# Q and K of an attention and SwiGLU kernel by seven block products in a stage of their own, with nine gate/up steps a slot

## The chip, the cores and the metric

The kernel runs on one core of a Trainium2 chip. A core has five engines with a queue of instructions each: TensorE (PE in the profile, its weight loads PEld), VectorE (DVE), ScalarE (ACT), GpSimd (POOL) and SyncE (SP, which here only issues DMAs). The metric is the device time of one execution in microseconds (us). Before the change it is 822.46 us, the median of three runs (822.39 to 822.51).

## The reference

`x` is one sequence of 2048 rows with 512 columns. Two branches read it, and a gate of one number a row mixes them:

```python
qkv = (x @ wqkv)                     # 32 heads of 16 columns for each of q, k, v
scores = q @ k.T * 16 ** -0.5        # kept where 0 <= row - column < 256, else -1e9
a = softmax(scores) @ v @ wo         # attention branch
b = (silu(x @ w_gate) * (x @ w_up)) @ w_down    # 1792 hidden units
g = sigmoid((x * gate_w).sum(-1, keepdims=True))
out = g * a + (1 - g) * b
```

Everything is float32.

## The kernel before, in words

All large products are split products: each operand is a high half (rounded to the float32r type) and a low half (the rest), and high x high, high x low and low x high are added up: three matmuls for each 128 rows of the contraction. `split` (L65) makes the halves: one cast, on ACT nearly everywhere, and one subtraction on POOL or DVE. x is held transposed in four chunks of 512 rows (`xhi`, `xlo`), so a product of x with 128 columns of weights is 4 x 3 = 12 matmuls a chunk.

The 32 heads are eight groups of four. The order of all work is written out by hand: each engine does its instructions in the order in which the program issues them, and waits are added where data or buffers ask for it.

*The front* (L370 to L500). x and the weights of V come in; Q and K of groups 0 and 1 and V of all 16 blocks of 128 rows are computed. V goes to DRAM (`vd`) and is fetched in pieces later. The last 12 blocks of V run as `lanes` (L211): a matmul over 128 rows is cut into two over 64, which run side by side in the two halves of the array, two results at a time, in a first and a second turn. Between them stand the first-stage scores of group 0.

*The attention loop* (L598). It has 128 slots (group, block of 128 keys) with four ticks each, one for each head, and a last slot for what is left. In a tick PE does:
- one score matmul of the next group (`stage1`, L263, line L275 in the profile), whose largest value DVE takes with the mask added (L277) into a buffer `ps1`;
- one score matmul of this group (`stage2`, L303, L314) into `ps2`, from which ACT makes the exponent (L316), and POOL clears what the window excludes (L318, L321);
- three steps of `lanes` (L225), two matmuls a step: a unit of 48 steps takes four slots. There are 32 units: Q and K of groups 2 to 7, and 26 of the 28 column blocks of gate and up. Their results are copied by ACT (L522), those of gate and up go to DRAM (`raws`).

Every fourth slot, after its second tick, come the value sums of 512 queries (`av`, L326, L338): one result of `pb` and one of `ps2` are filled. `finish` (L345) adds the two on DVE, transposes, divides by the row sums, transposes back and writes to DRAM (`od`), a piece a tick or so, within the next four slots.

`ps1`, `ps2`, `pa` and `pb` are four pairs of result buffers of 128 x 512. Each name turns over its two buffers, so an instruction that takes one waits until the reader of the buffer's last content is done.

In the last group there is no next group: both scores of two ticks are issued together, DVE makes halves of `wd` in the freed Q and K buffers (`wd_early`, L558), the gate is computed (L551 to L565), and the first hidden tile is prepared (`tile0`, L586).

*The second half* (L632). For each chunk of 512 rows and each of 14 blocks of hidden units: load the kept gate and up (`load_kept`, L685), silu and product (`hidden`, L691), halves (`halved`), and 12 matmuls (`step`, L716) which add to four results of 128 x 512. The one pair of gate and up that was not computed in the loop is computed here, 24 matmuls for each chunk (L700). Between steps stand the 16 blocks of attention times `wo` (`attn_out`, L661). The loads of `wd` and `wo` fall in the first chunk.

Of the kernel before, what the change touches and what calls it, by code (L numbers as in the profile page):

```python
# [9 lines left out]
F32 = mybir.dt.float32  # L10
# [23 lines left out]
def gated_mix(ctx, tc, xT, xn, wqk, wv, wo, wgu, wd, gw, out):  # L34
# [13 lines left out]
    od = dram.tile([G, P, S], F32, name="od")  # L48

    gate = const.tile([P, NB], F32, name="gate")  # L50
    igate = const.tile([P, NB], F32, name="igate")
    xhi, xlo = [], []
# [3 lines left out]


    ring = ctx.enter_context(tc.tile_pool(name="ring", bufs=2))
# [12 lines left out]

    def fetch(src, raw=None):

        raw = ring.tile([P, D], F32, name="raw", bufs=1) if raw is None else raw
        nc.sync.dma_start(raw, src)
        return raw
# [23 lines left out]


# [7 lines left out]
    QT = [[slot(f"q0{pr}") for pr in range(2)]]  # L109
    KT = [[slot(f"k0{pr}") for pr in range(2)]]  # L110


    WT = {}

    def products(key, c):
        wh, wl = WT[key]
        return [(wt[:, k], xt[c][:, k]) for k in range(NK) for wt, xt in ((wh, xhi), (wh, xlo), (wl, xhi))]

    def swapped(todo):

        return [todo[n] for k in range(0, len(todo), 3) for n in (k, k + 2, k + 1)]

# [3 lines left out]
    def weights(key, raw=None, lo_eng=nc.gpsimd):  # L126

        raw = fetch(weights_of(key), raw)

        def halves():  # L130
            hi, lo = (ring.tile([P, D], F32R, name=w) for w in ("wh", "wl"))
            WT[key] = by_k(hi), by_k(lo)
            split(hi, lo, raw, nc.scalar, lo_eng)
        return halves

    early = [("f", f, i) for f in range(NF - 1) for i in range(2)]
    KEPT = {(f, i, c) for _, f, i in early for c in range(NCH)}
    UNITS = []  # L140
    for g in range(2, G):
        UNITS += early[:2] + [("p", g)] + early[2:3]
        early = early[3:]
    UNITS += early
    raws = dram.tile([NF - 1, 2, NCH, P, CH], F32, name="raws")

    WD = {}
    ORDER = [0, NF - 1, *range(1, NF - 1)]

    WKEYS = list(UNITS)  # L150
    WKEYS += [("f", NF - 1, i) for i in range(2)]
    PEND = []
# [5 lines left out]
    def prepare():  # L158

        PEND.pop(0)()  # L160
        prefetch()

# [6 lines left out]
    pp = ctx.enter_context(tc.tile_pool(name="pp", bufs=2, space=PSUM))  # L169
    ps1 = ctx.enter_context(tc.tile_pool(name="ps1", bufs=2, space=PSUM))  # L170
    ps2 = ctx.enter_context(tc.tile_pool(name="ps2", bufs=2, space=PSUM))


    with ExitStack() as A:
        sm = A.enter_context(tc.tile_pool(name="sm", bufs=2))


        warm = pp.tile([P, CH], F32, name="pa")
        for _ in range(11):
            nc.tensor.matmul(warm[:, :P], ident, ident, start=True, stop=True)  # L180

        mask = sm.tile([P, 3 * P], F32, name="mask", bufs=1)
        nc.gpsimd.memset(mask, 0.0)
        nc.gpsimd.affine_select(out=mask, in_=mask, pattern=[[-1, 3 * P]], compare_op=ALU.is_ge,
                                fill=NEG, base=W, channel_multiplier=1)
        nc.gpsimd.affine_select(out=mask, in_=mask, pattern=[[1, 3 * P]], compare_op=ALU.is_ge,
                                fill=NEG, base=-1, channel_multiplier=-1)
# [4 lines left out]
        X = {}  # L192

        def x_pair(pool=None, name="x"):
            return tuple((pool or sm).tile([P, 2 * CH], F32R, name=f"{name}{w}", bufs=1) for w in ("hi", "lo"))

        def split_qk(g, hf, cc, raw):
            hi, lo = (t[:, cc * CH:(cc + 1) * CH] for t in X[g, hf])
            split(hi, lo, raw, *act)
# [617 lines left out]
```

## Time and profile before

| what | us |
|---|---|
| median of the runs | 822.46 |
| profiled execution, first to last instruction (its span) | 821.5 |
| front: up to the first attention slot | 79.5 |
| groups 0 to 6 of the attention loop | 455.0 |
| the last group | 61.9 |
| the second half, with the last value sums | 225.1 |

For the profiled execution the page gives no time but its span. In a row of the timeline the numbers are the start, the length, the engine, the line, the operation, what it writes and reads, how many rows were merged, and in brackets the idle time before it and what ended that. In a row of the groups they are count, total busy us, mean ns of one, and idle time before. In the chain they are start and length. A matmul's length overlaps that of its neighbours, so the pitch is read from starts.

### The profile page before, as it was taken

What the parts mean: (1) busy time and instruction counts of PE and PEld (TensorE: products, weight loads), DVE (VectorE), ACT (ScalarE), POOL (GpSimd) and SP (SyncE); (2) the same over time, 40 slices, a digit from 0 to 9 for tenths busy, and PEclk for the clock granted to TensorE, in tenths of its full rate; (3) what the DMA queues carried; (4) which work ended last, traced back from release to release, by engine and by line L of the source; (5) the groups of instructions that cost most, each with busy time, mean ns of one, the idle gap of its engine ahead of it and who ended that gap; (6) DMA issues with size and microseconds to landing.
All of it is one profiled execution on the core that took longest, in us unless ns stands there. A gap on an engine that the chain in (4) does not pass through costs nothing.

```text
span 821.5 us, 21573 instructions
## 1 busy us (share of the span) xinstructions
PE 815.1 (99%) x8329; PEld 683.8 (83%) x8329; DVE 515.6 (63%) x1437; ACT 448.9 (55%) x936; POOL 351.8 (43%) x640
## 2 busy tenths in 40 slices
PE   8999999999999999999999999999999999999998
PEld 7888988888888888888888888888887888888886
DVE  6397677677667676677677667756567453443543
ACT  6422666666656666666666666656654433333341
POOL 7812555555546555645554655456511221011020
PEclk9999999999999999999999999999999999999999
DMA  8574534624534543552562463466698563383531
GB/s 294 164 206 150 154 121 125 191 94 146 166 128 125 161 146 117 152 170 101 144 193 102 126 191 125 160 207 201 210 325 267 182 197 110 131 244 107 178 125 51
DMA packets 67957, 133.26 MB, mean 162 GB/s; under 512 B 11600, under 2 KB 16336, under 8 KB 67856
## 3 DMA queue, kind: packets, MB, share of 16 engines
q1 hardware_dynamic: 63888, 118.00, 46.3%
q0 software_dynamic: 3968, 13.90, 4.6%
q8 instruction: 65, 1.06, 0.6%
q14 instruction: 36, 0.29, 0.1%
HBM read 61.08 MB, written 45.61 MB: 130 GB/s over the span
## 4 chain that ended last, share of the span: by engine, by line
PE 95%; DMA 2%; DVE 1%; ACT 1%; issue 1%; SPq 0%; DVEq 0%; ACTq 0%
PE pb L225 24%; PE pa L225 24%; PE pb L338 7%; PE ps L275 6%; PE ps L87 5%; PE ps L85 5%; PE ps L86 5%; PE ps L314 5%; PE pb L205 2%; PE pa L205 2%; PE pb L85 2%; PE pb L87 2%; PE pb L86 2%; PE ps L338 2%; DMA got<-raws 1%; PE pb L700 1%
## 5 line engine op out<-in xcount | busy, mean ns | idle before, releaser
L277 DVE CUSTOM_DVE_ANT_0 ps<-ps,mask 128x384 f32<-128x384 f32 (+2 forms) x512 | 271.6, 539 | 143.2 <-PE ps L314 66.7
L316 ACT ACTIVATE pt<-ps 128x384 f32<-128x384 f32 (+2 forms) x512 | 240.7, 477 | 114.9 <-PE ps L275 57.7
L318 POOL TENSOR_SCALAR_AFFINE_SELECT pt<-pt 128x256 f32<-128x256 f32 x256 | 107.4, 419 | 223.8 <-ACT pt L316 220.4
L314 PE MATMUL ps<-q,k 64*128 64x384 f32 (+2 forms) x512 | 159.9, 329 | 0.0
L275 PE MATMUL ps<-k,q 63*128 63x384 f32 (+2 forms) x512 | 158.7, 330 | 0.0
L225 PE MATMUL pb<-xhi,wh 64*128 64x512 f32 x512 | 111.3, 394 | 0.0
L225 PE MATMUL pb<-xlo,wh 64*128 64x512 f32 x512 | 110.1, 391 | 0.0
L225 PE MATMUL pb<-xhi,wl 64*128 64x512 f32 x512 | 109.9, 392 | 0.0
L225 PE MATMUL pa<-xhi,wh 64*128 64x512 f32 x512 | 109.0, 394 | 0.0
L225 PE MATMUL pa<-xhi,wl 64*128 64x512 f32 x512 | 107.9, 391 | 0.0
L225 PE MATMUL pa<-xlo,wh 64*128 64x512 f32 x512 | 107.8, 391 | 0.0
L275 PEld LDWEIGHTS ps<-k,q 63*128 63x128 f32 x512 | 88.8, 185 | 16.9 <-issue 5.7
L321 POOL TENSOR_SCALAR_AFFINE_SELECT pt<-pt 128x256 f32<-128x256 f32 x224 | 98.7, 441 | 0.0
L314 PEld LDWEIGHTS ps<-q,k 64*128 64x128 f32 x512 | 89.9, 184 | 5.4 <-issue 0.8
L704 DVE TENSOR_TENSOR sg<-got,sg 128x512 f32<-128x512 f32 x51 | 45.1, 885 | 64.6 <-ACT sg L703 59.9
L338 PE MATMUL ps<-pt,vg 64*32 64x320 f32 (+4 forms) x1408 | 75.0, 346 | 0.0
L338 PE MATMUL pb<-pt,vg 64*32 64x320 f32 (+3 forms) x1360 | 73.9, 350 | 0.0
L277 DVE DVE_READ_ACCUMULATOR2_ANT mx<- 128x1 f32 x512 | 71.9, 140 | 0.0
L338 PEld LDWEIGHTS pb<-pt,vg 64*32 64x32 f32 x1360 | 46.4, 106 | 28.3 <-ACT pt L316 9.9
L225 PEld LDWEIGHTS pb<-xhi,wh 64*128 64x128 f32 x512 | 56.6, 185 | 7.9 <-ACT ev L522 0.3
L225 PEld LDWEIGHTS pb<-xhi,wl 64*128 64x128 f32 x512 | 56.5, 184 | 6.7
L225 PEld LDWEIGHTS pa<-xhi,wl 64*128 64x128 f32 x512 | 54.7, 184 | 7.4
(159 smaller groups left out, 1576.6 us busy)
## 6 DMA issues: line engine op xcount, KB each, us to landing
raws<-ev SPq DMA_DIRECT2D x104, 256.0 KB
got<-raws SPq DMA_DIRECT2D x102, 256.0 KB
od<-o POOLq DMA_DIRECT2D x32, 256.0 KB, 2.6
raw<-wgu SPq DMA_DIRECT2D x28, 256.0 KB
q<-xhi SPq DMA_DIRECT2D x56, 128.0 KB
k<-xhi SPq DMA_DIRECT2D x56, 128.0 KB
vd<-vs POOLq DMA_DIRECT2D x8, 672.0 KB, 5.1
vg<-vd SPq DMA_DIRECT2D x32, 168.0 KB
```

The source lines that it names most:

```text
L85: nc.tensor.matmul(ps, lh, rh, start=start and i == 0, stop=False, skip_group_check=skip)
L86: nc.tensor.matmul(ps, lh, rl, start=False, stop=False, skip_group_check=skip)
L87: nc.tensor.matmul(ps, ll, rh, start=False, stop=stop and i == n - 1, skip_group_check=skip)
L225: mm = nc.tensor.matmul(ps[me], w[r], x[r], start=not second and i == 0, stop=bool(second) and i == n - 1)
L275: nc.tensor.matmul(ps[:, :n], QT[g % 2][pr][r, q0:q0 + P], KT[g % 2][pr][r, k0:k0 + n], start=True, stop=True)
L277: mx = nc.vector.tensor_tensor_reduce(out=ps[:, :n], in0=ps[:, :n], in1=mask[:, 3 * P - n:], scale=1.0, scalar=NEG, op0=ALU.add, op1=ALU.m ...
L314: nc.tensor.matmul(ps[:, :n], KT[g % 2][pr][r, k0:k0 + P], QT[g % 2][pr][r, k0:k0 + n], start=True, stop=True)
L316: BEHIND.append(nc.scalar.activation(pt[:, j, :n], ps[:, :n], AF.Exp, scale=SCALE))
L318: nc.gpsimd.affine_select(out=pt[:, :, :P], in_=pt[:, :, :P], pattern=[[0, 2], [1, P]], compare_op=ALU.is_ge, fill=0.0, base=0, channel_mu ...
L321: nc.gpsimd.affine_select(out=pt[:, :, 2 * P:], in_=pt[:, :, 2 * P:], pattern=[[0, 2], [-1, P]], compare_op=ALU.is_ge, fill=0.0, base=-1, ...
L338: nc.tensor.matmul(AV[g, c][h][32 * j:32 * j + 32, q0 - c * CH:q1 - c * CH], VG[4 * g + kb // 4][o, kb % 4, 17 * j:17 * j + 32], PT[g, kb, ...
L704: nc.vector.tensor_tensor(out=sg, in0=gu[1], in1=sg, op=ALU.mult)
```

## The change

- V of all 16 blocks comes first, in full-array matmuls. Then Q and K of all groups are computed in a stage of their own: for two groups (256 columns of weights) and 1024 rows of x, four block results of 128 x 512 come from seven products of sums of blocks instead of eight products of blocks. The sums of x blocks are made on DVE while V runs, those of weight blocks during the products. Results are added up in the banks, with ACT copies (`copied`) and DVE additions (`add_to`) in between; their halves go to DRAM (`xd`) and are fetched by `stack` later. The gate's row sums move into this stage.
- The first-stage scores of group 0 then run beside four units of gate and up, in 64 ticks of three steps.
- The attention loop holds gate and up only (24 units): nine steps a slot (2, 2, 2, 3) instead of twelve. All 28 column blocks are computed before the second half, and L700 goes.
- The value sums use a buffer of `ps1` and one of `ps2`. `evacuate` frees both at once: ACT copies one, DVE the other, POOL adds them. The transposes and divisions run four slots later (`finish`).
- Two hidden tiles (not one) are prepared in the last group, and the third is loaded there.

```diff
+    PRODS = {1: ("a", 0, "B11"), 2: ("a", 1, "B21"), 6: ("s", 0, 2), 5: ("s", 1, 1),
+             7: ("s", 2, 3), 3: ("s", 3, "B22"), 4: ("z", 0, 4)}
...
+    def product(p, n, a):
...
+        for k in range(2):
+            w = slice(k * P, k * P + P)
+            for m, (l, r) in enumerate(((wh, xh), (wh, xl), (wl, xh))):
+                nc.tensor.matmul(ps, l[:, w], r[:, k], start=n in (1, 2, 5) and k == m == 0,
+                                 stop=k == 1 and m == 2, skip_group_check=True)
+        c = 2 * a
+        if n == 1:
+            copied((1, a), ps)
...
+        elif n == 2:
+            add_to(UT[1, a], ps)
+            put_c(p, 0, c, UT[1, a], False)
...
+        else:
+            put_c(p, 1, c, ps, True)
...
+        order = [(n, a) for n in ((1, 2, 6, 5, 7, 4, 3) if last else (1, 2, 6, 5, 7, 3, 4)) for a in range(2)]
+        for i, (n, a) in enumerate(order):
+            product(p, n, a)
+            if i < 8 and i % 2 == 0:
+                gate_fetch(4 * p + i // 2)
+            if i in (4, 6, 8, 10):
+                gate_block(4 * p + i // 2 - 2)
...
         def av(g, c):
-            AV[g, c] = (pp.tile([P, CH], F32, name="pb" if 4 * g + c + 1 < len(UNITS) else "pa"),
-                        ps1.tile([P, CH], F32, name="ps1") if 4 * g + c + 1 >= 4 * (G - 1) else ps2.tile([P, CH], F32, name="ps2"))
+            AV[g, c] = (ps1.tile([P, CH], F32, name="ps1"),
+                        ps1.tile([P, CH], F32, name="ps1") if g == G - 1 or g == G - 2 and c == NCH - 1
+                        else ps2.tile([P, CH], F32, name="ps2"))
...
+        def evacuate(g, c):
...
+            nc.scalar.copy(b[:, lo:], second[:, lo:])
+            nc.vector.tensor_copy(e, first)
+            if lo:
+                nc.gpsimd.memset(b[:, :lo], 0.0)
+            nc.gpsimd.tensor_tensor(out=b, in0=e, in1=b, op=ALU.add)
...
+                n = (k + 1) * 9 // 4 - k * 9 // 4
+                if t < G * NB:
+                    run(steps, n)
+                tick_end()
+                if hd == 1 and part == 0 and t:
+                    av(*divmod(d - 1, NCH))
                     run(FIN, 1)
-                if hd == 1 and part == 0:
+                    evacuate(*divmod(d - 1, NCH))
+                if hd == 3 and part == 0:
+                    run(FIN)
...
-                ps = pp.tile([P, CH], F32, name=name)
-                todo = products(("f", f, i), c)
-                for n, (w, x) in enumerate(todo):
-                    nc.tensor.matmul(ps, w, x, start=n == 0, stop=n == len(todo) - 1)
...
-        fresh, waiting, ready = [], [(0, 0, *TILE0)], []
+        fresh, waiting, ready = [], [(0, n, *TILE[n]) for n in range(2)], []
```

More of the change, by code (lines that the diff above doesn't have):

```diff
@@ L107, in halves_of @@
         return [t[:, :n], t[:, n:]]
[L109 to L121, printed above, removed]
     def weights_of(key):
         return wqk[key[1]] if key[0] == "p" else wgu[key[1], :, key[2]]
-    def weights(key, raw=None, lo_eng=nc.gpsimd):
-        raw = fetch(weights_of(key), raw)
+    UNITS = [("f", f, i) for f in range(NF) for i in range(2)]
@@ L167, in load_wd @@
         return lambda: split(*WD[f], raw, *dve)
[L169 to L171 removed]
     with ExitStack() as A:
         sm = A.enter_context(tc.tile_pool(name="sm", bufs=2))
[L178 to L187, printed above, removed]
+        osb = A.enter_context(tc.tile_pool(name="osb", bufs=1))
@@ L197, in split_qk @@
[L197 to L211 removed]
+        BEHIND, AT, NOW = [], {}, [0]
```

657 lines of the change are left out of this document (379 added, 278 removed).

## The prediction, made before the changed kernel had run

> **What bounds the kernel now.** I read the page first, then busy time by stretch, the chain that ended last, the groups of instructions with their shapes kept apart, and the timeline at four places.
>
> ```profile
> span 821.5 us, 21573 instructions
> PE 815.1 (99%) x8329; PEld 683.8 (83%) x8329; DVE 515.6 (63%) x1437; ACT 448.9 (55%) x936; POOL 351.8 (43%) x640
> ```
>
> PE is busy for 99% of the span, so the time is the number of matmuls times their pitch, as long as nothing holds them up. The sum below is made against this span, 821.5 us. The median of the three runs, 822.46 us, lies 0.96 us above it, and I carry those 0.96 us over unchanged.
>
> ```profile
> 13.28 10.88 PE pb L205 x48
> ...
> 549.05 1.39 PE pb L225 x12
> 550.44 0.17 PE ps L314 x2
> ```
>
> Three prices come from this piece of the chain. A matmul over all 128 rows takes 10.88 / 48 = 0.2267 us (called a full one). Two matmuls over 64 rows each, side by side in the two halves of the array, take 1.39 / 6 = 0.2317 us (a pair). A pair of score matmuls takes 0.17 us. In the attention loop one tick holds a score pair and three pairs of gate/up work: 0.17 + 3 x 0.2317 = 0.87 us.
>
> ```profile
> 205.56:270.90 65.34, 65.34 (x867) 55.21 (x866) 46.32 (x153) 41.98 (x93) 35.76 (x72) 1.00 0.47 144
> ...
> 597.00:625.00 28.00, 28.00 (x202) 22.76 (x187) 20.19 (x35) 14.68 (x26) 3.13 (x3) 1.00 0.89 310
> ```
>
> The columns are the stretch, its length, busy time of PE, weight loads, DVE, ACT and POOL, granted clock, DMA share and GB/s. The first row is one group of four heads (16 slots, 64 ticks): 65.34 us, of which DVE works 46.32 and ACT 41.98. So both have room, at this pitch. The second is the beginning of the second half (the sum over the hidden units): there the DMA engines are 0.89 busy at 310 GB/s.
>
> **The change, part by part.**
>
> *Matmuls.* Q and K cost 8 groups x 4 chunks x 12 = 384 full equivalents before and 4 x 2 x 7 x 6 = 336 after: 48 fewer. The rest is only moved. Full ones: 240 before (96 of Q and K, 48 of V, 96 of the last gate/up pair at L700) and 192 + 336 = 528 after: +288 x 0.2267 = +65.3 us. Pairs: 32 units x 48 + 144 of V = 1680 before and 28 x 48 = 1344 after: -336 x 0.2317 = -77.9 us. Sum **-12.6 us**, if PE never waits more than before. All other terms are waits.
>
> *The start: 0.* Before, 24 matmuls had been done by 13.28 us (row above): 13.28 - 5.44 = 7.8 us lost.
>
> ```profile
> 10.70 2.50 ACT L67 CAST wvh<-ev 128x512 fp32r<-128x512 f32 x4 [0.89 <-DMA ev<-wv]
> ...
> L70 POOL TENSOR_TENSOR wl<-raw,wh 128x512 fp32r<-128x512 f32 x34 | 44.5, 1310 | 2.9 <-ACT wh L67 2.9
> ```
>
> The four V weights had landed by about 12.5 us, behind 1.5 MB. Now only 1 MB of x goes with them, so the last lands near 12; its cast (0.6), the subtraction on POOL (1.31) and 12 matmuls (2.72) end V's first 48 matmuls near 18 us, which is 7.2 to 7.5 us lost. I take 0 (-1 to +1).
>
> *From V to the seven products: +1.5 (0 to 4).*
>
> ```profile
> L70 DVE TENSOR_TENSOR wl<-ev,wh 128x512 fp32r<-128x512 f32 x1 | 0.7, 692 | 1.5 <-ACT wh L67 1.5
> L70 DVE TENSOR_TENSOR wvl<-ev,wvh 128x512 fp32r<-128x512 f32 x2 | 3.0, 1476 | 1.5 <-ACT wvh L67 1.5
> ```
>
> Behind V's block 12 stand on DVE one subtraction of 512 columns, four sums of 256, one of 1024, one of 256 and four differences of 1024: about 14.5 x 0.69 = 10 us, and a wait of about 1.2 for ACT in between. ACT then casts 1024 columns (1.2) and only after that copies the first product (0.6). That is 13 us. PE has three blocks (8.2) and four products (5.4) = 13.6 until the sixth product overwrites the bank that this copy reads. The cover is 0.6 us, and the second row shows that a DVE subtraction beside one of POOL takes twice as long; POOL subtracts here. So I take 1.5.
>
> *The products' stage and DMA: +1.5 (0 to 8).*
>
> ```profile
> GB/s 294 164 206 150 154 121 125 191 94 146 166 128 125 161 146 117 152 170 101 144 193 102 126 191 125 160 207 201 210 325 267 182 197 110 131 244 107 178 125 51
> ...
> raws<-ev SPq DMA_DIRECT2D x104, 256.0 KB
> xlo<-xn SPq DMA_DIRECT2D x16, 256.0 KB
> 12.00:35.00 23.00, 23.00 (x104) 18.79 (x102) 12.23 (x14) 15.43 (x28) 19.48 (x21) 1.00 0.74 251
> ```
>
> A pair of groups takes 84 x 0.2267 = 19.0 us of PE. In that time eight results of 512 KB go to DRAM (each twice a transfer of the `raws` row), four blocks of x for the gate come in (the `xn` row), and 0.5 MB of weights: 5.8 MB, or 302 GB/s. The trace shows 310 at a share of 0.89, 251 at 0.74 and 325 in the best fortieth of the span, so it just fits. At 310 it costs nothing, at 251 it would be 23 us a pair of groups, +4 x 4 = 16 us; I take a value near the busier row, with a little for bunching, as six of the eight results leave in the last third and have four buffers. ACT, in order, holds the split behind a full buffer, and behind it the copy on which PE waits, four products later.
> The Trainium skill ("DMA: Bandwidth & Descriptors", section Bandwidth) measured 341 GB/s for transfers of 1 MB and 425 for 16 MB. By that this term would be 0; the best 20 us of this trace stand at 325.
>
> *Entry into attention: +0.5 (0 to 2).*
>
> ```profile
> L395 POOL MEMSET k<- 128x1024 f32 x8 | 7.4, 958 | 0.0
> ```
>
> The last Q/K rows are copied behind a memset (0.96) and two subtractions (1.3 each) on POOL, and SP stands behind that; the first score matmul comes seven ticks (4.9 us) after the last product. The gate's 16 row sums move into the products' stage; with them DVE has some 13 us of work in each 19 (about 19 operations of 512 columns at 0.69), so they cost nothing there.
>
> *The attention loop, 9 steps a slot instead of 12.* Ticks have 2, 2, 2 and 3 pairs: 0.17 + 2 x 0.2317 = 0.64 us, three times, and 0.87.
>
> ```profile
> 244.53 0.44 PE L275 MATMUL ps<-k,q 63*128 63x384 f32 x1
> 244.65 0.59 ACT L353 COPY o<-ps 128x512 f32<-128x512 f32 x1 [2.60 <-PE ps L338]
> 245.00 0.57 DVE L277 CUSTOM_DVE_ANT_0 ps<-ps,mask 128x384 f32<-128x384 f32 x1 [2.94 <-PE ps L314]
> 245.13 0.50 ACT L316 ACTIVATE pt<-ps 128x384 f32<-128x384 f32 x1
> 245.51 0.33 PE L275 MATMUL ps<-k,q 63*128 63x384 f32 x1
> 246.38 0.34 PE L275 MATMUL ps<-k,q 63*128 63x384 f32 x1
> ```
>
> This is the tick after a block of value sums. The next one starts 0.98 us later, then 0.87: the first tick after value sums is 0.1 us longer than a plain one. Scores have two buffers a stage, so a score matmul waits for the reduction (ps1) or the exponent (ps2) of two ticks earlier. In a plain tick (245.51 to 246.09, and a lag of about 0.4) the reduction is over some 0.95 us after its matmul began, and two short ticks are 1.28 us. So a plain tick does not wait.
>
> ```profile
> 8.62 0.50 PE L205 MATMUL pa<-xhi,wh 128*128 128x512 f32 x1 [0.49 <-ACT xhi L67]
> 8.95 0.39 PE L205 MATMUL pa<-xhi,wl 128*128 128x512 f32 x1
> ```
>
> A matmul that did wait loads its weights only then: the pitch is 0.33 instead of 0.227, so each wait costs 0.1 us more.
>
> Now the value sums take one buffer of ps1 and one of ps2 (before, pb and ps2), and DVE's copy frees the ps1 one.
>
> ```profile
> L355 DVE TENSOR_TENSOR o<-pb,o 128x512 f32<-128x512 f32 x23 | 15.8, 689 | 8.8 <-ACT o L353 8.6
> L69 DVE CAST q<-raw 128x512 fp32r<-128x512 f32 x4 | 1.7, 422 | 1.6 <-DMA got<-raws 1.6
> ```
>
> The trace has no DVE copy of 512 columns out of PSUM; its bounds are 0.42 (a cast from SBUF) and 0.69 (an add from PSUM). I take 0.69, the row with the same source. The copy ends 0.13 + 0.69 = 0.82 us after the tick behind the sums began, and the matmul can go at 0.82 + 0.05 + 0.1 = 0.97. It is due at 0.98 - 0.23 = 0.75 us, since that tick has two pairs. So 0.22 to 0.24 us are lost at each of 27 blocks: **+6.5** (0 to 10). At 0.42 ACT's copy (0.12 + 0.59) is the later one, and 0.12 x 27 = 3 us are lost. The divisions, four slots later, run under the value sums, where DVE had nothing; the last transpose delays two reductions by less than the slack.
> The Trainium skill ("VectorE: DVE Perf Modes", Mode 2x_2P) says that a one-source fp32 operation gets two elements a cycle only between SBUF operands, because PSUM has one read port. By that the copy is near 0.69 and the term 6.5; by the SBUF row it would be 3.
>
> *Copies of gate/up results: +1 (0 to 5).*
>
> ```profile
> L522 ACT COPY ev<-pb 128x512 f32<-128x512 f32 x64 | 37.7, 590 | 0.5 <-PE pb L225 0.5
> ```
>
> Two now come in neighbouring ticks. Exponent plus copy is about 0.9 us of ACT in a tick of 0.64, so the exponents fall 0.55 us behind, which two buffers and the long tick just absorb; where the cast of the next weights follows at once (8 of 24 units), 0.1 to 0.2 is lost.
>
> *The last group (no first-stage scores): +3.3 (0 to 6).*
>
> ```profile
> 545.51 0.42 PE L314 MATMUL ps<-q,k 64*128 64x384 f32 x2
> 545.96 0.88 ACT L316 ACTIVATE pt<-ps 128x384 f32<-128x384 f32 x2 [0.62 <-PE ps L314]
> ```
>
> Both score buffers are filled at once, and the second exponent is over 1.33 us later; with 0.15 of release and weight load the next pair's second matmul goes at 1.48. It was due at 1.64 (six pairs) and is now due at 1.18 (four) or 1.41 (five): 0.3 lost in each of some 11 slots without value sums.
>
> *The second half: +4 (0 to 6).*
>
> ```profile
> 640.86 2.72 PE pa L700 x12
> 643.58 2.72 PE pb L700 x12
> ...
> 609.70 0.43 DVE L69 CAST q<-raw 128x512 fp32r<-128x512 f32 x1 [1.56 <-DMA got<-raws]
> ...
> 626.63 0.39 PE L86 MATMUL ps<-q,hh 128*128 128x512 f32 x1
> 627.37 0.50 PE L87 MATMUL ps<-q,hl 128*128 128x512 f32 x1 [0.36 <-DVE hl L70]
> ```
>
> The 24 matmuls of L700 are gone four times (already counted). The first time they also gave loads 5.4 us to run ahead, and even so PE waits 0.5 us at 626.6 for a chain of loads at 310 GB/s. Three tiles instead of one come from earlier, against two that needed no load before: one pair of loads less, 0.52 MB / 0.31 = 1.7 us. 5.4 - 1.7 = 3.7 us of wait, plus some 0.8 at the first sum, which now finds its banks just being copied, less slack won back: 4.
>
> *Sum.* -12.6 + 0 + 1.5 + 1.5 + 0.5 + 6.5 + 1 + 3.3 + 4 = +5.7: a span of 827.2 us and a time of **828 us**.
>
> **Rivals.**
>
> *The loop's waits do not bite* (PE's queue has enough ahead, the copies are quicker): the three loop terms are 0 and the rest stays, -12.6 + 7.5 = -5, 817 us; with a free second half too, 813. For it: DVE works 46.3 of 65.3 us in a group and would work about as much of 54.2, so there is room on average. Against it: two buffers and 0.64 us leave little room at one place.
>
> *Half of them bite:* 3 + 0.5 + 1.6 in the loop gives about 0, 822 us.
>
> *DMA binds the products' stage:* it decides if the writes to DRAM get less than 300 GB/s. At 251 the term is 16 instead of 1.5: 842 us; at 275, 834.
>
> *Every short tick waits:* if release takes 0.1 us longer than I think, each of 7 x 48 short ticks could lose 0.1: 828 + 34 = 862. Against it: that DVE's reductions follow one another within 0.6 us.
>
> *It does not do what it says:* the number of PE instructions tells it (48 matmuls fewer).
>
> **How the numbers follow.** Forecast (824 to 834): 0.40. Loop does not wait (813 to 820.8): 0.37. Parity: 0.09. DMA binds (834 to 842): 0.10. Every tick waits: 0.04. A measurement of this kernel can tell about 0.2% (1.6 us) from no change. Faster 0.37, same 0.09, slower 0.54. For 8 in 10 the range runs from 813 to 838; the forecast's own range is 824 to 834.
>
> **What would show it.** A group of heads at 54.2 us between equal places says that the loop does not wait; 55.5 to 56 says the value sums cost what I think. The tick after the sums should be 0.97, not 0.75. A products' stage of 76 us says DMA does not bind; over 80, it does. PE gaps waiting for `hl` at the third to eighth step of the second half are worth 4 us; in the last group they are gaps before every other score pair. I am wrong if the copy out of PSUM takes 0.45 us, if PE stalls somewhere that I hold covered (between V and the products, or SP behind POOL at the entry), or if the loads of the second half start earlier than the last value sums.

## The result and the profile after

The changed kernel takes **858.5 us** (median of four runs, 857.0 to 867.4) where the kernel before takes 822.5: 1.046 times as long (95% interval 1.041 to 1.051). The forecast was 828.0 with a range to 838. The profiled run took 856.95 us, its span 855.0; the forecast span was 827.2, so 27.8 us are to be found.

From the page of the changed kernel, the span, the first engine's row and PE's granted clock in fortieths of the span:

```profile
span 855.0 us, 21084 instructions
...
PE 824.7 (96%) x7945; PEld 681.3 (80%) x7945; DVE 589.3 (69%) x1503; ACT 465.2 (54%) x947; POOL 385.6 (45%) x671
...
PEclk9898999799999999999999999999999999999999
```

PE, busy for 99% of the span before, is now busy for 96%, and its clock dips in three places, all in the first fifth. Busy time by stage (V; the seven products; the 64 ticks ahead of attention; attention; second half), with the columns of the prediction:

```profile
0.00:57.97 57.97, 51.61 (x215) 42.18 (x216) 30.73 (x32) 26.46 (x42) 21.18 (x28) 0.94 0.52 177
57.97:143.50 85.53, 78.52 (x338) 63.93 (x336) 52.06 (x88) 41.08 (x70) 43.81 (x30) 0.96 0.73 254
143.50:204.68 61.18, 52.51 (x451) 44.37 (x450) 39.64 (x136) 11.17 (x21) 18.44 (x18) 0.92 0.70 234
204.68:650.80 446.12, 444.35 (x6079) 368.87 (x6079) 362.16 (x1108) 302.16 (x669) 272.81 (x572) 1.00 0.47 153
650.80:855.00 204.20, 197.69 (x867) 161.97 (x867) 104.70 (x145) 84.28 (x146) 29.32 (x23) 1.00 0.61 193
```

The first three rows are where PE idles and the clock is below 1.00. V's 192 matmuls should fill 192 x 0.2267 = 43.5 us after a start at 6.4, and the stage ends 8.1 us later than that. The products' 336 should fill 76.2, and take 9.3 more. The ticks take 52.35 in experiment 8 below, where one short stop is left, and 8.8 more here. That is 26.2 us, for which the forecast had allowed 3.5 (1.5 + 1.5 + 0.5); about 5 more lie in attention and behind.

Each loss is one or two stops of PE and the slower matmuls behind them. A stop is counted below from the start of one matmul to the start of the next. The timeline of the changed kernel at the first:

```profile
23.93 0.59 ACT L183 COPY vs<-ps 128x512 f32<-128x512 f32 x1 [5.26 <-DMA vd<-vs]
24.41 1.14 ACT L67 CAST xhi<-k 128x512 fp32r<-128x512 f32 x2
...
25.07 1.29 DVE L70 TENSOR_TENSOR xlo<-k,xhi 128x512 fp32r<-128x512 f32 x2 [9.36 <-ACT xhi L67]
...
30.95 6.08 DVE L70 TENSOR_TENSOR xlo<-k,xhi 128x512 fp32r<-128x512 f32 x2
...
33.83 0.79 PE L208 MATMUL pa<-wvh,xlo 128*128 128x512 f32 x1 [3.09 <-DVE xlo L70]
```

Read it upwards: PE waits for a low half of x, the low half stands on DVE behind four differences, these behind a cast on ACT, and the cast, which needed nothing that was late, behind a copy that waits 5.26 us for a buffer of V. At the second stop:

```profile
70.62 0.33 SPq L312 DMA_DIRECT2D gwb<-gw  x1
71.11 0.80 SPq L127 DMA_DIRECT2D rw<-wqk  x2
...
76.04 0.62 ACT L67 CAST ah<-rw 128x512 fp32r<-128x512 f32 x1 [6.80 <-DMA rw<-wqk]
76.57 0.61 ACT L67 CAST cx<-u 128x512 fp32r<-128x512 f32 x1
77.09 0.58 ACT L373 COPY u<-pb 128x512 f32<-128x512 f32 x1
...
70.66 0.40 PE L389 MATMUL pa<-q,sl 128*128 128x512 f32 x1
77.72 1.22 PE L389 MATMUL pb<-k,sh 128*128 128x512 f32 x2 [6.66 <-ACT u L373]
78.74 0.63 PE L389 MATMUL pb<-k,sl 128*128 128x512 f32 x1
79.17 1.05 PE L389 MATMUL pb<-k,sh 128*128 128x512 f32 x2
```

The gate weights (`gwb`) go out at 70.62 only, because their memory is that of V's last blocks; the weights of the next products stand behind them on SP, ACT's cast behind these, and the copy that frees PE's bank behind the cast: 7.06 us. SP's waits of the whole run hold the first link, 56.0 us in 5 waits:

```profile
SPq L312 <- DMA vd<-vs: 56.0, 5, 23.3
```

The third stop (8.78 us from 149.16) ends with the first reduction of scores:

```profile
144.05 1.28 DVE L369 TENSOR_TENSOR u<-ps,u 128x512 f32<-128x512 f32 x2
153.01 3.00 DVE L326 TENSOR_SCALAR gate<-gate 128x16 f32<-128x16 f32 x1 [7.68 <-ACT gate L325]
...
157.53 0.30 DVE L559 CUSTOM_DVE_ANT_0 ps<-ps,mask 128x128 f32<-128x128 f32 x1 [0.61 <-DMA xd<-cx]
```

I read this as the gate's closing work standing ahead of the reduction. The bracket of the last row (a transfer of the copied heads) seemed small; it is the clue that I passed over.

### The profile page after: what moved, and what is told of

Its sections match the earlier page's. It is cut to its first block, busy times and chain, and to the rows that moved or that the text cites. A ratio compares the mean times of both kernels' runs of the same rounds, so it can differ in the third digit from the quotient of the medians.

```text
span 855.0 us, 21084 instructions
## 1 busy us (share of the span) xinstructions
PE 824.7 (96%) x7945; PEld 681.3 (80%) x7945; DVE 589.3 (69%) x1503; ACT 465.2 (54%) x947; POOL 385.6 (45%) x671
## 4 chain that ended last, share of the span: by engine, by line
PE 87%; DMA 5%; issue 3%; DVE 3%; SPq 1%; ACT 1%; POOL 1%; DVEq 0%; ACTq 0%; POOLq 0%
PE pa L514 18%; PE pb L514 18%; PE ps L620 9%; PE ps L557 7%; PE ps L81 5%; PE ps L80 5%; PE ps L79 5%; PE ps L596 5%; PE ps L389 3%; PE pb L389 2%; PE pa L389 2%; PE pb L80 2%; PE pb L81 2%; PE pb L79 2%; DMA vd<-vs 1%
## 5 line engine op out<-in xcount | busy, mean ns | idle before, releaser
L559 DVE CUSTOM_DVE_ANT_0 ps<-ps,mask 128x384 f32<-128x384 f32 (+2 forms) x512 | 271.6, 543 | 45.2 <-PE ps L557 34.3
L596 PE MATMUL ps<-q,k 64*128 64x384 f32 (+2 forms) x512 | 172.0, 347 | 0.8 <-ACT pt L598 0.7
L514 PE MATMUL pa<-xhi,wh 64*128 64x512 f32 x448 | 101.1, 399 | 8.6 <-DVE mx L559 8.6
L514 PE MATMUL pb<-xhi,wh 64*128 64x512 f32 x448 | 101.5, 394 | 0.0
L514 PE MATMUL pb<-xlo,wh 64*128 64x512 f32 x448 | 100.2, 393 | 0.0
L514 PE MATMUL pb<-xhi,wl 64*128 64x512 f32 x448 | 99.3, 391 | 0.0
L514 PE MATMUL pa<-xhi,wl 64*128 64x512 f32 x448 | 98.8, 395 | 0.0
L620 PEld LDWEIGHTS ps<-pt,vg 64*32 64x32 f32 x2816 | 50.7, 106 | 29.3 <-issue 8.4
L637 POOL TENSOR_TENSOR ob<-oe,ob 128x512 f32<-128x512 f32 x32 | 42.1, 1317 | 68.0 <-DVE oe L634 66.7
L559 DVE DVE_READ_ACCUMULATOR2_ANT mx<- 128x1 f32 x512 | 72.3, 141 | 0.0
L514 PEld LDWEIGHTS pa<-xhi,wh 64*128 64x128 f32 x448 | 52.4, 188 | 12.1 <-DVE mx L559 8.8
L67 ACT CAST hh<-sg 128x512 fp32r<-128x512 f32 x54 | 33.3, 617 | 42.9 <-PE ps L80 27.0
```

The lines of the kernel that those rows point to most:

```text
L514: mm = nc.tensor.matmul(ps[me], w[r], x[r], start=not second and i == 0, stop=bool(second) and i == n - 1)
L559: mx = nc.vector.tensor_tensor_reduce(out=ps[:, :n], in0=ps[:, :n], in1=mask[:, 3 * P - n:], scale=1.0, scalar=NEG, op0=ALU.add, op1=ALU.m ...
L596: nc.tensor.matmul(ps[:, :n], KT[g % 2][pr][r, k0:k0 + P], QT[g % 2][pr][r, k0:k0 + n], start=True, stop=True)
L620: nc.tensor.matmul(AV[g, c][h][32 * j:32 * j + 32, q0 - c * CH:q1 - c * CH], VG[4 * g + kb // 4][o, kb % 4, 17 * j:17 * j + 32], PT[g, kb, ...
```

## The experiments

My theory after the result: the 28 us are these three stops and the half-rate matmuls behind them, each by an in-order queue in front of a wait. Rivals: the stops only move elsewhere, or the loss lies in the loop or in the DMA rate. The runs of the changed kernel spread over 10.4 us and those of the other kernels over up to 5.4, so differences of 2 us or less between totals decide nothing; a time below that has no interval or ratio beside it is that of a single run.

**1. The order of the fetches.**
```
-    nc.sync.dma_start(gwb, gw[None, :].to_broadcast([P, D]))
...
             RW[p + 1] = pair_fetch(PAIRS[p + 1])
+        if p == 0:
+            nc.sync.dma_start(gwb, gw[None, :].to_broadcast([P, D]))
+        fetch_at, block_at = ((5, 7, 9, 11), (8, 10, 12, 13)) if p == 0 else ((0, 2, 4, 6), (4, 6, 8, 10))
```


> In the products' stage the load of the gate weights is issued behind the next head pair's weights, and the first pair's four gate fetches four to five steps later. Nothing is left out. My theory (the sync engine works in order, the gate weights wait for memory that the last T blocks of V still hold, and the next weights stand behind them): the 7.06 us stop of the matmuls at 70.66 goes, and with it the 1.2 us that the matmuls behind it lost at half rate; about 8 us less than the changed kernel, 848 to 850 us. First rival (the stage is bound by the rate of its transfers, and the stop is only where that shows): the wait moves to another step of the stage, which then lasts 83 us or more instead of 77, and the time falls by under 3 us, 854 to 857. Second rival (the time lost sits in the attention loop): as the first, 3 us or less.

850.3 us. The 7.06 us stop is gone, the stage takes 82.07 instead of 85.53:

```profile
58.24:140.31 82.07, 78.18 (x337) 62.28 (x335) 54.67 (x89) 40.64 (x70) 45.04 (x30) 1.00 0.78 273
```

PE's clock is 1.00 throughout, at a DMA rate of 273 GB/s rather than 254. The stop was the order on SP. But only 3.5 us came back in this stage, where I had expected it to last 77: shorter stops, of up to 1.7 us each, took part of its place.

**2. V's casts first.**
```
+        if b < 6:
+            v_extra(b)
         put_v(b, ps)
-        v_extra(b)
+        if b >= 6:
+            v_extra(b)
```


> In the V stage the casts and differences of x for blocks 4 and 5 are issued ahead of the copy that waits for a buffer of V's way to HBM. Nothing is left out. My theory (the scalar engine works in order, the casts stand behind a 5.26 us wait for the transfer of a V block, and the differences behind the casts): the two stops of 3.48 and 2.23 us at 30.35 and 34.85 go, and the half-rate matmuls up to 40.24 with them (about 2 us); 7 to 8 us less than the changed kernel, 848.5 to 850. First rival (the two subtractions of 6.08 us on the vector engine, beside those of GpSimd, are the cause by themselves): the stop of 2 to 3.5 us stays with them, and the time falls by 3 us or less. Second rival (the V stage's end only moves the same wait into the products' stage, whose memory waits for the same transfers): the V stage is shorter by 7 us and the stop of 7.06 us grows by as much; the time stays within 2 us of 857.

851.5 us. V ends at 50.26 instead of 57.97, both stops gone; the stop in the products stayed (6.97 us). The two subtractions that had taken 6.08 us take 1.29 in their new place, so this run cannot part the queue from the slow subtractions. By the row of the changed kernel both count: issued at 30.95 and made in 1.29 us, the two would have ended at 32.24, while they ended at 37.03. By that estimate the late cast alone would have stopped PE for about 1 us; that the subtractions were slow because POOL subtracted beside them was not tested.

**3. The gate's closing work at tick 44** (`gate_end()` moved from the end of the products' stage into the tick loop).

> The gate's closing work (exponential, square root, selection) is issued at the 44th of the 64 ticks behind the products' stage instead of ahead of the first. Nothing is left out. My theory (the first tick that follows the opening ones stands on a reduction that stands on the vector engine behind the gate's closing work): the stop of 8.78 us at 149.16 shrinks to 1 us or less and the half-rate matmuls behind it go; 8 to 10 us less than the changed kernel, 847 to 849 us. First rival (the casts of the copied heads, which the scalar engine can do only when their buffers come free behind a transfer, hold the reductions all the same): 3 to 5 us of the stop stay, time 851 to 854. Second rival (the same gate work costs as much where it now stands, in the run-in of attention): the stop goes there and the time stays within 2 us of 857.

858.8 us: nothing. The stop is 8.72 us, and with the gate out of the way the waits of that stretch (total us, number, longest) name another lock, that is, something else for which the same instruction has to wait:

```profile
DVE ps L558 <- DMA xd<-cx: 12.3, 1, 12.3
```

**4. All three.**

> All three changes of order together: the gate weights behind the next weights, the casts of x ahead of V's copies, the gate's closing work at the 44th tick. Nothing is left out. My theory (27 of the 28 us by which the changed kernel missed what its matmuls and their known waits add up to are these three stops and the half-rate matmuls behind them, one apart from the other): about 829 us, 826 to 833, and a ratio to the kernel before of 1.004 to 1.012; attention's loop and the second half as in the changed kernel (55.95 us a group of heads, 200 us). Rival (the stops only move on, or the loss lies in the loop): over 845 us.

846.7 us, 1.030 (1.027 to 1.033): the two that worked, and a stop of 9.54 us where the third was. My theory of the third stop had fallen.

**5. The row maxima in memory of their own.** The reduction writes a 128-byte tile in a pool whose memory the copied heads' buffers held.
```
-                MX[g, hf] = sm.tile([P, 4, NB // 2], F32, name="mx")
+                MX[g, hf] = const.tile([P, 4, NB // 2], F32, name=f"mx{hf}")
```
With experiment 4, and alone in the changed kernel:

> The three changes of order, and the tile of row maxima (128 bytes a partition, two of them) in memory of its own, where it stood in memory that the stage of the products leaves. Nothing is left out. With the gate moved the stop of 9.54 us at 137.15 was still there; the trace now names the transfer xd<-cx as what the first reduction waited for, 13.1 us. My theory (the reduction writes into memory that the copied heads' buffers held, and so waits for the last of their transfers to land; the gate was a second lock on the same door): the stop goes down to 1 us or less, and the half-rate matmuls behind it go; 11 to 12 us less than the three orders alone, 832 to 836 us, and 1.012 to 1.017 of the kernel before. Rival (the reduction waits for the copied heads themselves, which the scalar engine delivers late, or for a bank of PSUM): the stop stays over 6 us and the time over 842.

> The changed kernel with the tile of row maxima in memory of its own and nothing else. Nothing is left out. My theory (two locks on the same reduction, of which the gate's closing work, done on the vector engine by 156.5, opens hardly earlier than the transfer that lands at about 157): the stop of 8.78 us at 149.16 shrinks by 1 to 2 us only, 855 to 858 us. Rival (the memory alone held the reduction, and the gate's work does not): the stop goes, 846 to 849 us.

846.6 us (1.029, 1.027 to 1.031) and 856.8, the second as expected. The memory theory was right and the expected time wrong: the reduction came at 137.03, but PE then stopped 2.35 us for a copy and 7.43 us for the low halves of the next weights.

```profile
PEld pa L518 <- POOL wl L70: 7.5, 1, 7.5
...
ACT ev L535 <- DMA xd<-cx: 4.0, 1, 4.0
```

The copy writes memory that the last transfer leaves; the low halves stood on POOL behind a row of twelve fills of 0.9 us. The four locks stand in parallel, so opening one at a time shows nothing.

**6. The tail off the queues** (on experiment 5).
```
-                if i == 11:
+                if i == 13:
                     stack(0, 0, (1,))
...
-        for hf in range(2):
-            constant_rows(hf, 1, ("q10", "k10", "q11", "k11"), nc.gpsimd)
...
+            if n in (9, 11, 13, 15):
+                constant_rows((n - 9) // 4, 1, (("q10", "k10"), ("q11", "k11"))[n // 2 % 2], nc.gpsimd)
+            if n == 18:
                 stack(1, 0)
```


> As the kernel with the maxima in memory of their own, and: the second half of the first stacking is issued behind all but two of the copied heads' transfers (it stood ahead of five), and the eight fills of the second group's rows go to ticks 9 to 15 (they stood, with four others, in one row of 10.7 us on GpSimd ahead of the second unit's low halves), its stacking to tick 18. Nothing is left out. My theory (with the reduction freed, the same late tail of the products' stage held the matmuls at its next doors: 2.35 us for the copies into memory that the last transfer xd<-cx leaves, 7.43 us for the low halves behind the fills; then half-rate matmuls): both stops go to 1 us or less each and the matmuls stay at full rate; 10 to 13 us less, 832 to 836 us, first value sums' loop from 182 us instead of 194. Rival (the low halves wait for their raw weights, or the next wait in line takes the place again): a stop of over 5 us stays and the time is over 841.

840.0 us (1.021, 1.019 to 1.023): 6.6 of the 10 to 13 us. Both stops went, and one of 3.13 us took their place, a score waiting for its stacked rows (`PE ps L559 <- DMA k<-xd` in the waits).

**7. The loop's 1.75 us a group.** First a longer tick behind the value sums (on experiment 5):
```
-                n = (k + 1) * 9 // 4 - k * 9 // 4
+                n = ((k + 1) * 9 + 1) // 4 - (k * 9 + 1) // 4
```


> As the kernel with the maxima in memory of their own, and the tick of three gate and up steps, one in four, set right behind the value sums. Nothing is left out. My forecast put 0.24 us on each of 27 blocks of value sums, because the tick behind them waits for its copies out of PSUM; a group of heads took 55.95 us where its matmuls fill 54.2. If that wait is what fills the difference, the third step covers most of it: a group of 54.6 to 55.2 us and 5 to 7 us less than with the maxima alone. Rival (the difference is spread over all ticks, or the three steps' own tick is late wherever it stands): within 1.5 us of it.

847.6 us (1.032, 1.030 to 1.034). Then, on experiment 6, the last transpose five ticks later, with the splits of the down weights one step later in the second half; and on top of that the copy on ACT, or left out:
```
-                if hd == 3 and part == 0:
+                if hd == 3 and (part == 1 or t == G * NB):
                     run(FIN)
...
-            nc.vector.tensor_copy(e, first)
+            nc.scalar.copy(e, first)
```
(without the copy, `nc.gpsimd.memset(e, 1.0)` stands in its place)

> As the kernel with the tail off the queues, and two moves: in the loop, the second transpose of the divided value sums goes five ticks later, to a tick of three steps, off the vector engine's queue right behind the sums; in the second half, the splits of the down weights are issued one step later. Nothing is left out. My theory of the loop (moving the long tick changed nothing, since the 1.75 us a group are a backlog of the vector engine behind the sums: a copy of 0.69, reductions at 0.6 to 0.7 and a transpose of 0.71 without a pause from 320.4 to 325.1 against ticks of 0.64): without the transpose in that place 0.1 to 0.2 us of each 0.44 go, a group of 55.2 to 55.6 us instead of 55.95, 3 to 5 us in all; the second half loses one stop of 2.3 us for the split that stood ahead of the halves. Together 4 to 7 us less. Rival for the loop (the wait is for the sums' own copies out of PSUM, 0.24 us each): the group stays at 55.9.

> As the kernel with the last turn later, and the copy of the value sums' first bank is made by the scalar engine, ahead of that of the second, instead of by the vector engine. Nothing is left out. My theory (backlog of the vector engine): another 0.69 us leaves its queue behind each of 28 blocks, and the group goes on down to 54.5 to 55.0 us, 3 to 5 us less than the kernel with the last turn later. Rival (the scalar engine, 37.8 us busy in a group of 56, takes over as the late one, since its exponentials of 0.49 stand behind 0.6 more): the group stays within 0.2 us or grows.

> The kernel with the last turn later, but the vector engine's copy of the value sums' first bank is left out: half of each block's sums never reaches the output, and GpSimd fills its place with ones without waiting for the matmuls. The bank comes free with the matmuls themselves. My theory (what is left of the loop's loss, 55.70 us a group against 54.2 of matmuls, is the 0.69 us copy: the score behind it finds its bank late, and the vector engine starts the next ticks that much behind): a group of 54.3 to 54.8 us, 829 to 833 us in all. Rival (the reductions of 0.6 to 0.7 against ticks of 0.64 are late by themselves, sums or not): 55.3 us or more.

839.1 us (1.021, 1.019 to 1.022), 849.6 (1.034, 1.032 to 1.036) and 833.6. One group of heads each, in this order: the changed kernel, the longer tick, the later transpose, the copy on ACT, no copy.

```profile
313.70:369.71 56.01, 56.00 (x771) 46.55 (x769) 47.29 (x154) 37.81 (x83) 34.11 (x73) 1.00 0.50 161
```
```profile
303.29:359.31 56.02, 55.76 (x770) 46.64 (x768) 47.55 (x153) 37.62 (x84) 33.65 (x72) 1.00 0.49 161
```
```profile
296.46:352.23 55.77, 55.76 (x771) 46.40 (x769) 47.23 (x154) 37.90 (x83) 34.19 (x73) 1.00 0.49 161
```
```profile
297.36:354.42 57.06, 56.80 (x770) 48.76 (x768) 43.94 (x150) 39.83 (x87) 34.12 (x73) 1.00 0.48 158
```
```profile
293.46:348.75 55.29, 55.29 (x772) 48.70 (x770) 43.93 (x150) 37.85 (x83) 36.04 (x77) 1.00 0.52 163
```

The longer tick gains nothing, so my account of a wait that one more step would cover fell. These are single groups. The starts of the first-stage scores give the mean slot of groups 1 to 6, in us; the first row is an estimate, from ticks of 0.63 and 0.87 and the 2.54 us that a block of value sums took in the kernel before:

| | slot with value sums | second | third | fourth | group |
|---|---|---|---|---|---|
| without waits | 5.31 | 2.77 | 2.77 | 2.77 | 54.4 |
| changed kernel | 5.54 | 2.83 | 2.83 | 2.79 | 56.0 |
| longer tick | 5.46 | 3.00 | 2.78 | 2.78 | 56.0 |
| later transpose | 5.52 | 2.77 | 2.88 | 2.77 | 55.7 |
| copy on ACT | 5.91 | 2.77 | 2.83 | 2.79 | 57.2 |
| no copy | 5.45 | 2.77 | 2.83 | 2.79 | 55.4 |

So the longer tick took 0.08 us off the slot with the sums and put 0.17 on the next. The transpose is worth 0.23 us a group and the copy 0.35 (0.09 a block of sums, a good third of what I put on it); moved to ACT it costs 1.4 us a group, as that rival had it. With both out, 1.0 us a group remains, most of it in the slot with the sums and the third; what holds PE there is open. The later splits left the second half as long as it was, 204.6 us.

**8. Without the gate** (on experiment 7's later transpose).

> The kernel with the last turn later, without the gate's work in the products' stage: its 17 loads and 16 reductions are left out and the gate's sums are set to zero. The products' stage lasts 81.3 us now where 336 matmuls of 0.2267 make 76.2. My theory (the vector engine, in order, stands behind xn's loads, 24.3 us in all, and with it the sums that open the banks of the next products): the stage goes to 77 to 78.5 us, and with the loads gone the copied heads leave earlier, so the stop of 3.07 us behind it shrinks too; 832 to 836 us. Rival (the stage's rest is the weights' splitting and the banks alone): 80 us or more, time over 837.

830.0 us. The products' stage is 77.0 us and PE's clock 1.00 in it and in the 64 ticks behind it, which take 52.35:

```profile
50.66:127.70 77.04, 76.68 (x337) 62.72 (x335) 45.22 (x57) 41.25 (x70) 43.20 (x31) 1.00 0.65 234
127.70:180.05 52.35, 50.41 (x450) 47.49 (x449) 35.05 (x133) 11.53 (x21) 18.44 (x18) 1.00 0.82 263
```

**9. The gate in the last group**, near where the kernel before had it: its fetches and blocks two ticks apart in the last rows' memory, in experiment 7's kernel with the later transpose (the mended kernel) and alone in the changed one.
```
+        at(4 * g7, put_pieces, gate_place)
+        for b in range(NB):
+            at(4 * g7 + 1 + 2 * b, lambda b=b: gate_fetch(b))
+            at(4 * g7 + 3 + 2 * b, lambda b=b: gate_block(b))
+        at(4 * g7 + 33, gate_leave, gate_end)
```


> The kernel with the last turn later, and the whole of the gate's work (17 loads, 16 reductions, the closing work) goes out of the products' stage to the first 33 ticks of the last group of heads, in the memory of the zeroth parity's last rows. Nothing is left out. My theory (without the gate the products' stage took 76.7 us instead of 81.3 and the whole kernel 830.0; in the last group the vector engine has no row maxima to take, so the same work hides there): products' stage 76.5 to 77.5 us, the last group no longer by more than 1 us, 829 to 832 us, 1.009 to 1.012 of the kernel before. Rival (the last group, which has its own wait, pays for the loads and the reductions): as much as 5 us come back there, 833 to 836.

> The changed kernel with the gate's work in the last group and nothing else. Nothing is left out. My theory (the gate's loads are what stands on the sync engine's queue in the products' stage, the gate weights' wait for V's memory first of all; the two stops in V, the maxima's memory and the row of fills are other causes): the stop of 7.06 us goes, the stage takes 77 to 79 us instead of 85.4; V's stops of 3.48 and 2.23 us and the stop of 8.78 us behind the stage stay within 2 us of what they were; 846 to 850 us. Rival (the gate's place is the one cause and the other stops follow from it): under 840.

849.7 us (1.033, 1.032 to 1.035) and 869.2. In both the products' stage fell to 77.0 us, in the changed kernel from 85.53 by this edit alone; V's stops and the one behind the stage stayed (3.37, 2.23 and 7.85 us), so the gate is one cause among several. But the last group paid more, and more than the 5 us of my rival: 74.6 us in the mended kernel, where it had taken 57.3. From the waits there:

```profile
DVE k L318 <- DMA k<-xn: 16.1, 9, 4.2
ACT ob L622 <- DVE ot L633: 12.8, 3, 9.8
PEld ps L585 <- ACT pt L587: 12.2, 13, 6.0
```

DVE waits in order for a block of x, ACT for DVE, and PE for the exponentials behind ACT's copy. With two fills and the stacking one step earlier on top (expected 828 to 830) it was 850.8, no better. With six buffers, so that loads are issued twelve ticks ahead:

> The kernel with the gate in the last group, with six buffers for its loads instead of two, so that each load is issued twelve ticks (some 8 us) ahead of the reduction that reads it, and the reductions at ticks 12 to 42; the last four early down weights go 20 ticks later to make room. Nothing is left out. My theory (two buffers left 1.4 us between a load and its reduction where the loads take more, the vector engine waited 16.1 us in order, the scalar engine's copy of the sums behind it 12.8 and the exponentials behind that): those waits go, the stops of 4.04 and 5.93 us with them, and the last group takes 56 to 58 us; with the products' stage at 76.7 that makes 829 to 833 us. Rival (the reductions themselves, or the down weights pushed late, are too much for the last group): stops of over 3 us stay there, 836 or more.

840.7 us (1.022, 1.020 to 1.024), and a last group of 67.1 us. The wait for blocks of x went, and one for the down weights, pushed late, took its place:

```profile
DVE q L69 <- DMA ev<-wd: 11.8, 1, 11.8
```

## Why the prediction was wrong

**Matmuls, -12.6, and the start, 0: right.** PE has 384 instructions fewer (8329 to 7945), which is 288 full matmuls more and 336 pairs of two fewer; the 48 of the prediction are full equivalents, not instructions. Where nothing stops PE, the products' 336 matmuls take 77.0 us against 76.2, and V's stage ends at 50.26. V's first 48 matmuls end near 18 us, as forecast.

**The gate in the products' stage, "they cost nothing there": the first failed step, by one load.** I compared DVE's work (13 us) with the stage (19 us a pair) and not the gate's loads with the queues they are issued on. Moving the gate out gave 85.53 to 77.00 us. By pairs of groups the changed kernel shows where the loss was:

```profile
57.97:86.28 28.31, 21.30 (x85) 16.82 (x84) 16.49 (x24) 12.24 (x19) 13.11 (x8) 0.88 0.49 153
86.28:105.33 19.05, 19.05 (x86) 15.77 (x85) 11.77 (x22) 9.60 (x17) 8.44 (x7) 1.00 0.83 296
105.33:124.36 19.03, 19.03 (x85) 15.77 (x84) 13.05 (x24) 9.61 (x17) 8.97 (x7) 1.00 0.84 307
124.36:143.50 19.14, 19.14 (x86) 15.58 (x84) 10.74 (x21) 9.62 (x17) 13.30 (x11) 1.00 0.87 308
```

The last three pairs have the gate's loads and row sums too, and take what 84 matmuls take, so there they did cost nothing. The whole loss is in the first pair: the 7.06 us stop behind the gate weights, the half rate behind it, and 0.6 us at the junction with V. With the order of experiment 1 some 5 us stay, and in the mended kernel too; its pairs take 21.9, 21.5, 19.1 and 19.2 us. Its longest stop in that stage ends so:

```profile
69.95 0.69 DVE L323 SCALAR_TENSOR_TENSOR junk<-xn,gwb 128x512 f32<-128x512 f32 x1 [3.13 <-DMA xn<-xn]
70.56 0.69 DVE L371 TENSOR_TENSOR u<-pb,u 128x512 f32<-128x512 f32 x1
71.30 0.73 PE L391 MATMUL pb<-k,zh 128*128 128x512 f32 x2 [1.77 <-DVE u L371]
```

A row sum of the gate waits for its block of x, the addition that frees PE's bank stands behind it, and PE behind that. The mean rate is not what holds the first two pairs back: they move 171 and 286 GB/s, and the two that lose next to nothing 305 and 322. Experiment 1's edit had also put the first pair's gate loads later; whether that made these new stops, no run tests.

**DMA, +1.5 (0 to 8): it cost nothing where it could be seen.** By the mark that I set ("over 80, it does") DMA would bind. It misled: 85.5 us came at 254 GB/s, but the last three pairs ran at full pace at 296 to 308, about the 302 that I had asked for.

**From V to the products, +1.5; V's own stage, no term: a failed step too, the first in time.** At the junction PE loses 0.6 us, at 63.91, to a copy on ACT; that is within the term. The loss lies in V, 7.7 us (experiment 2), where I had priced ACT and DVE behind block 12 but not ACT's copies waiting for V's two buffers, nor DVE's subtractions beside POOL's in that place, though one row of the prediction had them at twice the time.

**Entry into attention, +0.5 (0 to 2): the second failed step.** It cost about 9 us. I saw the stacking, the fills and SP, but costed them as durations; they are also locks: a 128-byte tile and the copies' buffers in memory that a transfer still holds, and twelve fills ahead of the next weights.

**The loop, +6.5, and copies of results, +1: too low.** Groups 0 to 6 of the changed kernel, by the starts of `stage2`'s scores:

```profile
204.68:593.45 388.77, 388.69 (x5279) 323.83 (x5281) 327.01 (x1056) 264.01 (x580) 235.74 (x501) 1.00 0.47 152
```

Before they took 455.0 us, and 336 pairs (77.9 us) are gone, so the waits cost about 11.5 us where the sum has 7.5. My sign of 55.5 to 56 us a group came true, but it stood above my own sum, which makes 54.2 + 4 x 0.24 + 0.15 = 55.3. The slot with the value sums lost the 0.24 us that I had put on it (5.54 for 5.31). What failed is "a plain tick does not wait": the other three slots lose some 0.15 us together, 0.6 a group. Part of it is the last transpose, which I had put within the slack: with the transpose later the second slot takes 2.77. DVE's copy takes 0.69 us as I chose:

```profile
L634 DVE COPY oe<-ps 128x512 f32<-128x512 f32 x32 | 22.1, 691 | 30.9 <-PE ps L620 30.9
```

But taking the copy out gives back 0.35 us a group, not the 0.96 that I put on it. That the sums' slot lost just what I had said is in part luck.

**Last group, +3.3, and second half, +4: right in size.** The last group, with the last value sums, takes 57.4 us. Before, it took 61.9 without them; less 48 pairs (11.1) and with a block of sums (2.5) that makes 53.3, so the waits are 4.1. The second half takes 204.2 us where 867 matmuls fill 196.6; PE's last ends at about 851, so some 3.5 us of the difference are waits and 4 the last results' way out. The kernel before had the way out too (its PE ends at 817.7 of 821.5), so 3.5 stands against the 4.

So the sum came close where I had followed a wait from end to end, and failed in the front, where I had shown that engines have room on average. The front took 22.7 us more than its terms, the loop 4, and the last group and the second half about what was said: some 27 of the 27.8. My rivals with a price were about the loop and the rate, none about an order; of the places where PE stopped only the entry stood in the last paragraph, among what would make me wrong. With the orders mended the kernel takes 839 us, with the gate's work left out 830, and no version here beats the kernel before.

## What to carry to other kernels

For a step that moves, write down for each queue what now stands behind its waits, memory that an earlier stage still holds included: an engine with time to spare on average still stops everything behind one late load. A stage that ends with several waits open at once shows only the last of them; undoing one proves little when the time stays, so look at what the trace names next and undo them together. And work moved to where its engine is idle can cost more than where it was: with its loads issued a tick or two ahead it waited for them, and with the loads issued twelve ticks ahead other loads came late.

## What the hardware showed that I had not expected

**Half rate after a stop.** Behind the 7.06 us stop matmuls start 0.43 us apart (78.74 to 79.17 above) instead of 0.23, until 81.2, so for 3.5 us. Every stop of 3.3 us or more in these runs did this, most for 3 to 7 us, so such a stop costs its length and half of that time, some 1.5 to 3.5 us, more. Shorter stops did it in some runs and not in others: one of 2.17 us did (experiment 4, up to 649.80), one of 3.24 us did not (experiment 7 with the copy on ACT, up to 142.86). The stages whose stops stayed under 2 us (the products in experiments 1 and 8, the ticks in 8) have a clock of 1.00. The Trainium skill ("TensorE: Matmul & The Clock Gate", Part 1: The HAM clock gate) gives half the clock after an idle window of some 3.4 us, until as much busy time has passed. The long stops agree with it; the stop of 2.17 us was shorter than that window and brought half rate all the same.

**A small operation on DVE beside a fill on POOL.** The gate's addition over 16 columns took 3.00 us at 153.01. POOL had begun a subtraction just before and then made two fills, 1.84 us in all; the addition ended with the second:

```profile
152.93 1.26 POOL L70 TENSOR_TENSOR cx<-u,cx 128x512 fp32r<-128x512 f32 x1 [3.27 <-ACT cx L67]
154.13 1.84 POOL L333 MEMSET q<- 128x1024 f32 x2
```

The same operation took 0.18 us in the last group (experiment 9), where POOL did nothing beside it. The Trainium skill ("GPSIMD Engine Reference", 1. Specifications) says that GpSimd's SBUF interfaces are shared with VectorE and contend with its two-port modes; that fits, but I did not test it by itself.
